# RWKV attention feeding a routed MoE on one core: TensorE's products of a unit reordered by array tiling, scores as quarters, rows from the state as column halves

## The chip, the cores and the metric

One core of one Trainium2 chip runs one program. The metric is the device time of one execution in microseconds (us). The kernel before takes 412.05 us (median of 3 runs, 411.41 to 412.96).

## The reference

```python
for t in range(S):                                   # B=4, H=8, S=768, D=48
    cur = np.einsum('bhd,bhe->bhde', u[None] * kt, vt)
    y[:, :, t] = np.einsum('bhd,bhde->bhe', rt, state + cur)
    state = wt[:, :, :, None] * state + np.einsum('bhd,bhe->bhde', kt, vt)
...
x = y.transpose(0, 2, 1, 3).reshape(B * S, H * D)    # 3072 rows of 384
logits = x @ w_gate + modality_bias[modality_id]     # 8 experts
e_idx = np.argmax(logits, axis=1)
...                                                  # gate_w: softmax value of that expert
for e in range(E):
    h = np.maximum(x[mask] @ w1[e], 0.0)             # 384 -> 1024
    out[mask] = gate_w[mask, None] * (h @ w2[e])     # 1024 -> 384
```

A recurrence over time with a decay per channel gives 3072 rows; each row then goes through the one expert that its logits choose.

## The kernel before

The sequence is cut into chunks of 128 steps. A **unit** is one chunk of one batch entry with all eight heads; there are 24, numbered n = 0 to 23, six to a batch entry. Channels lie on partitions, two heads to a tile (partitions 0 to 47 and 64 to 111), four such pairs side by side.

`att_iter(i)` (L222) works on three units at once. For unit a = i+2, VectorE (DVE) runs two scans over the decay, `B` (L230) and `E` (L233), and multiplies out `K` (L236) and `R` (L201). GpSimd (POOL) then writes `G` into the tile of `E` (L240; the profile calls it `E<-in`), after `R` has read it.

For unit m = i+1, TensorE (PE) transposes `K` into `pK` (L248), makes `delta(m)` (L213: what a step adds to its own row, four products into four column tiles of 32), the scores `pS` (L263), the state's transposed copy and update in `pU` (L273, L278), and the transposed `dl` (L280). DVE masks the scores into `A` (L269). ScalarE (ACT) copies PSUM tiles out: `KT`, `dl`, `xT`, `dT` and the state `SP`, `SPb` (L288, L291). POOL makes `dV` (L293) from `dT`. In the last unit of a batch entry there is no `pK`, no `SP` and no state update.

For unit z = i, PE makes the rows `pY` or `pX`: from the state (L303) and from the scores (L308). One iteration later DVE adds `dV` and writes `xb` (`x_rows`, L336). Two iterations later PE transposes `xb` (`x_cols`, L343) and multiplies by the gate (`logits`, L348), always into the one PSUM tile `pR_x`.

Every engine works through its own queue in the order in which the program is written (`manual_schedule`), so a waiting instruction holds up all behind it. `hooks` put extra work into an iteration after the scores: a setup at i = 4 and 5, and the routing of the first half at i = 14, 15 and 16 (`route_a`, `route_b`, `table`; the names `oh`, `tab`, `pR_x` in DVE's rows). From i = 15 to 20, POOL issues twelve scatters of `xb` (`drain`, L530), two at the end of each iteration, and at i = 18 to 20 five subtractions of the weight split (`wl`, L196) between `G` and `dV`. POOL's queue in such an iteration is `G(a)`, `wl`, `dV(m)`, scatter, scatter.

After unit 23 come the blocks of the MoE: `blk_t` (L559) transposes rows, `blk_up` (L571) and `blk_down` (L588) multiply. The last `x_rows`, `x_cols` and `logits` are put among the products of block 0.

A product's tiling follows from its operands: the rows of the array from the partitions of the operands (128, or 64 for the scores of a head), the columns from the output's partitions (128, 64 or 32). The profile prints it as rows*columns, as in `64*128`. Each fp32 product stands as two instructions.

Of the kernel before, what the change touches and what calls it, by code (L numbers as in the profile page):

```python
# [14 lines left out]
ALU = mybir.AluOpType  # L15
# [37 lines left out]
def kernel(ctx: ExitStack, tc: tile.TileContext, rkw, vt, wf, cst, mid, wg, bias, w1, w2, out):  # L53
# [107 lines left out]
    def setup_b():  # L161

        pm = pt("m", "pT")
        nc.tensor.transpose(out=pm[:, 0:NU], in_=mf, identity=ident[0:NU, 0:NU])
        m1 = cp.tile([P, 2, NU], F32, name="m1")
        nc.vector.tensor_copy(out=m1[:, 1], in_=pm[:, 0:NU])
        nc.gpsimd.tensor_scalar(out=m1[:, 0], in0=m1[:, 1], scalar1=-1.0, scalar2=1.0, op0=ALU.mult, op1=ALU.add)
# [42 lines left out]
    def delta(m):  # L210
        G, pU = T["G", m], T["pU", m]
        for p in range(4):
            nc.tensor.matmul(out=pU[32 * p:32 * p + 32, 256:384], lhsT=ub[:, p], rhs=G[:, p * P:(p + 1) * P],  # L213
                             start=True, stop=True, tile_position=(0, 32 * p))
        nc.scalar.copy(out=T["dl", m], in_=pU[:, 256:384])

# [5 lines left out]
    def att_iter(i):  # L222
# [18 lines left out]
        if ok(m):  # L241
            K, R, v = T["K", m], T["R", m], T["v", m]
            pU = pt(m, "pU")

            if not first(m + 1):
# [25 lines left out]
            cont = not first(m)  # L271
            if cont and not first(m + 1):
                nc.tensor.matmul(out=pU[:, 0:4 * D], lhsT=ident, rhs=T["SP", m].rearrange("p a b -> p (a b)"), start=True, stop=False,  # L273
                                 skip_group_check=True)
            for h in range(0 if first(m + 1) else H):
                p, hh = divmod(h, 2)
                c0 = p * P + 64 * hh
                nc.tensor.matmul(out=pU[64 * hh:64 * hh + 64, p * D:(p + 1) * D], lhsT=KT[:, c0:c0 + 64],  # L278
                                 rhs=v[:, h * D:(h + 1) * D], start=not cont, stop=True, skip_group_check=True)
# [3 lines left out]
            if not first(m + 1):  # L283
                pUv = pU[:, 0:4 * D].rearrange("p (a b) -> p a b", a=4)
# [25 lines left out]
        if ok(z - 2):  # L310
            logits(z - 2)
# [392 lines left out]
    for n, q in enumerate(seq):  # L704
# [239 lines left out]
```

## Time and profile before

| what | value |
|---|---|
| median of 3 runs | 412.05 us (411.41 to 412.96) |
| the profiled execution's own time | 411.19 us |
| its span, first to last instruction | 408.7 us |
| PE, DVE busy, share of the span | 93%, 65% |
| ACT, POOL busy, share of the span | 52%, 55% |
| mean granted TensorE clock | 0.957 |

The profiled execution lies 0.86 us under the median. Busy shares are means over two stages: the attention, up to about 174 us, where DVE and PE are both busy nearly throughout, and the MoE from there to about 401 us, where PE is. The granted clock is 1.0 at 2.4 GHz and 0.5 at 1.2 GHz.

### The profile page before, as it was taken

How to read it: one execution, taken by the hardware profiler on the slowest of the kernel's cores; microseconds unless marked ns; L12 is line 12 of the kernel's file. 1: busy time of each engine (PE TensorE's matmuls, PEld its weight loads, DVE VectorE, ACT ScalarE, POOL GpSimd, SP SyncE). 2: the span in 40 equal slices, each digit the busy share in tenths (PEclk: the TensorE clock that was granted, in tenths of full speed). 3: DMA queues.
4: the chain of work that ended last, by engine and by line, in shares of the span. 5: the costliest groups of instructions: out<-in, count | busy, mean ns of one | idle time of the engine just before them, and what ended most of it. 6: DMA issues, size and time to landing. Idle time of an engine off the chain costs nothing.

```text
span 408.7 us, 9897 instructions
## 1 busy us (share of the span) xinstructions
PE 381.1 (93%) x3807; PEld 353.6 (87%) x3807; DVE 266.5 (65%) x438; ACT 214.2 (52%) x452; POOL 224.0 (55%) x180
## 2 busy tenths in 40 slices
PE   5999979999795998999999999999999999999990
PEld 2688868888584887999999999999999999999990
DVE  5999999999988899566628684351725426471110
ACT  1354334435320554266746858777686776754320
POOL 3544263243244788158476989366484745738350
PEclk9599999999997999899999999999999999999996
DMA  7975756997636452600123653313124184146100
GB/s 155 212 161 132 166 121 128 269 248 171 157 82 153 119 136 79 197 2 1 40 59 131 239 153 119 116 42 98 54 83 132 38 289 162 40 147 194 67 28 20
DMA packets 17884, 50.46 MB, mean 123 GB/s; under 512 B 2853, under 2 KB 10571, under 8 KB 17828
## 3 DMA queue, kind: packets, MB, share of 16 engines
q1 hardware_dynamic: 14692, 40.28, 38.4%
q0 software_dynamic: 3136, 9.47, 6.4%
q8 instruction: 32, 0.52, 0.6%
q14 instruction: 24, 0.20, 0.2%
HBM read 72.89 MB, written 11.63 MB: 207 GB/s over the span
## 4 chain that ended last, share of the span: by engine, by line
PE 62%; DVE 25%; issue 5%; POOL 4%; DMA 2%; ACT 0%; SPq 0%; DVEq 0%; POOLq 0%; ACTq 0%
PE pS_u L571 23%; PE pX_d L588 12%; PE pY_d L588 12%; DVE B L230 6%; DVE E L233 5%; DVE A L269 5%; PE pS L263 3%; DVE R L201 3%; PE pR_x L348 2%; DMA in<-rkw 2%; DVE xb L336 2%; PE pK_x L559 1%; PE pT L343 1%; PE pX L308 1%; PE pX L303 1%
## 5 line engine op out<-in xcount | busy, mean ns | idle before, releaser
L196 POOL TENSOR_TENSOR wl<-raw,wh 128x768 fp32r<-128x768 f32 (+1 forms) x57 | 102.5, 1809 | 77.5 <-ACT wh L195 66.7
L195 ACT CAST wh<-raw 128x768 fp32r<-128x768 f32 (+1 forms) x104 | 83.2, 807 | 34.2 <-PE pX_d L588 24.3
L577 DVE SCALAR_TENSOR_TENSOR hl<-pS_u,hh 128x512 fp32r<-128x512 f32 x48 | 33.1, 690 | 90.7 <-ACT hh L576 90.6
L571 PE MATMUL pS_u<-xh,wh 128*128 128x256 f32 x288 | 82.0, 285 | 1.0 <-DVE hl L577 1.0
L571 PE MATMUL pS_u<-xo,wh 128*128 128x256 f32 x288 | 81.4, 283 | 0.0
L571 PE MATMUL pS_u<-xh,wl 128*128 128x256 f32 x288 | 80.9, 281 | 0.0
L240 POOL TENSOR_TENSOR E<-in 128x512 f32<-128x512 f32 x24 | 30.7, 1279 | 75.6 <-issue 23.9
L571 PEld LDWEIGHTS pS_u<-xh,wh 128*128 128x128 f32 x288 | 54.0, 188 | 1.4 <-DVE hl L577 1.4
L571 PEld LDWEIGHTS pS_u<-xh,wl 128*128 128x128 f32 x288 | 54.6, 190 | 0.0
L571 PEld LDWEIGHTS pS_u<-xo,wh 128*128 128x128 f32 x288 | 54.1, 188 | 0.0
L196 DVE TENSOR_TENSOR wl<-raw,wh 128x768 fp32r<-128x768 f32 (+1 forms) x47 | 51.2, 1089 | 2.8 <-ACT wh L195 1.8
L576 ACT ACTIVATE hh<-pS_u 128x512 fp32r<-128x512 f32 x48 | 28.8, 599 | 40.3 <-PE pS_u L571 36.4
L230 DVE TENSOR_TENSOR_SCAN B<-in,d1b 128x516 f32<-128x516 f32 x24 | 40.9, 1702 | 3.5 <-DMA in<-rkw 3.5
L596 POOL DMA_INDIRECT out<-ot,xl x25 | 32.3, 1294 | 10.9 <-ACTq L887 5.2
L588 PE MATMUL pY_d<-wh,hh 128*128 128x384 f32 x96 | 33.1, 345 | 0.0
L530 POOL DMA_INDIRECT xs<-xb,posT x24 | 28.3, 1181 | 7.9 <-issue 5.4
L263 PEld LDWEIGHTS pS<-R,K 64*128 64x128 f32 x384 | 27.3, 215 | 5.8 <-issue 4.3
L263 PE MATMUL pS<-R,K 64*128 64x128 f32 x384 | 32.3, 315 | 0.0
L269 DVE TENSOR_TENSOR A<-pS,cs 128x512 f32<-128x512 f32 x48 | 30.8, 682 | 2.2 <-PE pS L263 2.2
L588 PE MATMUL pX_d<-wh,hl 128*128 128x384 f32 x96 | 32.2, 335 | 0.0
L588 PE MATMUL pX_d<-wh,hh 128*128 128x384 f32 x96 | 32.1, 335 | 0.0
L588 PE MATMUL pX_d<-wl,hh 128*128 128x384 f32 x96 | 32.1, 335 | 0.0
(189 smaller groups left out, 751.7 us busy)
## 6 DMA issues: line engine op xcount, KB each, us to landing
raw<-w SPq DMA_DIRECT2D x56, 768.0 KB
in<-rkw SPq DMA_DIRECT2D x46, 288.9 KB
xl<-xs SPq DMA_DIRECT2D x12, 386.0 KB
v<-vt SPq DMA_DIRECT2D x24, 192.0 KB
wg<-wf SPq DMA_DIRECT2D x8, 576.0 KB
xs<-zt SPq DMA_DIRECT2D x8, 193.0 KB
out<-ot,xl POOLq DMA_INDIRECT x25, 3.1
xs<-zt SPq DMA_DIRECT2D x1, 386.0 KB
```

Of the source, the lines that this page charges most:

```text
L195: nc.scalar.copy(out=wh[k][:, sl], in_=raw[k][:, sl])
L196: (eng or (nc.vector, nc.gpsimd)[k]).tensor_tensor(out=wl[k][:, sl], in0=raw[k][:, sl], in1=wh[k][:, sl].bitcast(F32), op=ALU.subtract)
L230: nc.vector.tensor_tensor_scan(out=Bt[:, 516:0:-1], data0=w[:, 516:0:-1], data1=d1b[:, 516:0:-1], initial=0.0, op0=ALU.mult, op1=ALU.max)
L240: nc.gpsimd.tensor_tensor(out=G, in0=r, in1=k, op=ALU.mult)
L263: nc.tensor.matmul(out=pS[hh][:, p], lhsT=K[q, p], rhs=R[q, p], start=True, stop=True)
L269: nc.vector.tensor_tensor(out=A[:, hh], in0=pS[hh], in1=mask[:, None, :].to_broadcast([P, 4, P]), op=ALU.mult)
L530: rows_apart("xs", nc.gpsimd.indirect_dma_start(out=xs[:, :], out_offset=bass.IndirectOffsetOnAxis(ap=posT[:, n:n + 1], axis=0), in_=T["xb ...
L571: nc.tensor.matmul(out=pp[:, i], lhsT=wsrc[0][:, f, c * P:(c + 1) * P], rhs=xsrc[:, c], start=(n == 0), stop=(n == 3 * KC - 1))
L576: nc.scalar.activation(out=hh, in_=pp, func=AF.Relu)
L577: nc.vector.scalar_tensor_tensor(out=hl, in0=pp, scalar=0.0, in1=hh.bitcast(F32), op0=ALU.max, op1=ALU.subtract)
L588: nc.tensor.matmul(out=X["y", q][j], lhsT=hsrc[:, i, j * P:(j + 1) * P], rhs=wsrc[1][:, f], start=(f == 0 and n == 0), stop=(f == FC - 1 a ...
L596: ins = nc.gpsimd.indirect_dma_start(out=out[:, :], out_offset=bass.IndirectOffsetOnAxis(ap=xl[:, j, DM + 1:DM + 2].bitcast(I32), axis=0), ...
```

## The change

Within `att_iter`, PE's products of an iteration stand in another order: `K`'s transposes, `x_cols`, the state's copy (these with the whole array), then `delta` (128*32), the scores (now 64*64), the state update, the rows from the state and the rows from the scores (all 128*64), then the transposed `dl` and `logits` (whole array again). `x_cols` comes ahead of the scores; the transpose of `dl`, ACT's copy `dT` and POOL's `dV` come behind the rows. A score product of 64 rows by 128 columns is split into two of 64 by 64 into PSUM partitions 0 to 63 and 64 to 127, with the same 128 streamed columns (8 products become 16). A product of the rows from the state is split in the same way (4 become 8, each with 96 streamed columns). `delta` and the transposed `dl` go into the PSUM tile `pT` in place of `pU`; the setup's transpose goes into `pR_x` in place of `pT`.

```diff
@@ setup_b
-        pm = pt("m", "pT")
-        nc.tensor.transpose(out=pm[:, 0:NU], in_=mf, identity=ident[0:NU, 0:NU])
+        pm = rcol(C_VEC, NU)
+        nc.tensor.transpose(out=pm, in_=mf, identity=ident[0:NU, 0:NU])
@@ delta
-            nc.tensor.matmul(out=pU[32 * p:32 * p + 32, 256:384], lhsT=ub[:, p], rhs=G[:, p * P:(p + 1) * P],
+            nc.tensor.matmul(out=pT[32 * p:32 * p + 32, DM:], lhsT=ub[:, p], rhs=G[:, p * P:(p + 1) * P],
@@ att_iter
                 nc.scalar.copy(out=KT, in_=pK)
+            if ok(z - 2):
+                x_cols(z - 2, pT)
+
+            if cont and not last:
+                nc.tensor.matmul(out=pU[:, 0:4 * D], lhsT=ident, rhs=T["SP", m].rearrange("p a b -> p (a b)"), start=True, stop=False,
+                                 skip_group_check=True)
...
             for p in range(4):
-                for hh in range(2):
-                    q = slice(64 * hh, 64 * hh + 64)
-                    nc.tensor.matmul(out=pS[hh][:, p], lhsT=K[q, p], rhs=R[q, p], start=True, stop=True)
+                for s0 in (0, 64):
+                    for hh in range(2):
+                        q = slice(64 * hh, 64 * hh + 64)
+                        nc.tensor.matmul(out=pS[hh][s0:s0 + 64, p], lhsT=K[q, p, s0:s0 + 64], rhs=R[q, p], start=True, stop=True)
             if m == 0:
                 delta(0)
-            if ok(z - 2):
-                x_cols(z - 2)
...
-            nc.tensor.transpose(out=pU[:, 384:512], in_=T["dl", m], identity=ident)
-            dT = wt(m, "dT", [P, 4, 2])
-            nc.scalar.copy(out=dT, in_=pU[:, 384:512].rearrange("p (a b) -> p a b", a=4)[:, :, 0:2])
...
-            dV = wt(m, "dV", [P, H, D], 3)
-            nc.gpsimd.tensor_tensor(out=dV, in0=v.rearrange("p (a b) -> p a b", a=H),
-                                    in1=dT.rearrange("p a b -> p (a b)")[:, :, None].to_broadcast([P, H, D]), op=ALU.mult)
...
             if not first(z):
                 for p in range(4):
-                    nc.tensor.matmul(out=pY[:, 2 * p * D:2 * (p + 1) * D], lhsT=R[:, p], rhs=SPb[z % 3][:, p].rearrange("p a b -> p (a b)"),
-                                     start=(p == 0), stop=False, skip_group_check=True)
+                    for q in (0, 64):
+                        nc.tensor.matmul(out=pY[q:q + 64, 2 * p * D:2 * (p + 1) * D], lhsT=R[:, p, q:q + 64],
+                                         rhs=SPb[z % 3][:, p].rearrange("p a b -> p (a b)"),
+                                         start=(p == 0), stop=False, skip_group_check=True)
...
+        if ok(m):
+            pT = T["pT", m]
+            nc.tensor.transpose(out=pT[:, 0:P], in_=T["dl", m], identity=ident)
+            dT = wt(m, "dT", [P, 4, 2])
+            nc.scalar.copy(out=dT, in_=pT[:, 0:P].rearrange("p (a b) -> p a b", a=4)[:, :, 0:2])
+            dV = wt(m, "dV", [P, H, D], 3)
+            nc.gpsimd.tensor_tensor(out=dV, in0=T["v", m].rearrange("p (a b) -> p a b", a=H),
+                                    in1=dT.rearrange("p a b -> p (a b)")[:, :, None].to_broadcast([P, H, D]), op=ALU.mult)
         if ok(z - 2):
             logits(z - 2)
```

How PE's queue moves, in the iteration of unit m = 9 (after its scores, up to the next unit's transposes). Before:

```order
L343 MATMUL pT_993<-cs,xb_952 128x128 x3
L273 MATMUL pU_968<-SP_919,cs 128x192
L278 MATMUL pU_968<-v_860,KT_974 64x48 x8
L280 MATMUL pU_968<-cs,dl_976 128x128
L303 MATMUL pY_1022<-SPb_129,R_782 128x96 x4
L308 MATMUL pY_1022<-v_771,A_888 64x48 x16
L348 MATMUL pR_x<-cs,xT_994 128x8 x3
```

The same engine with the change, in the iteration of unit m = 8, from the last score product up to the next unit's first score product (the scores between are rows of the one kind):

```order
L272 MATMUL pS_8_983<-R_860,K_858 64x128
L281 MATMUL pU_960<-v_849,KT_967 64x48 x8
L300 MATMUL pX_1017<-SPb_128,R_740 64x96 x8
L306 MATMUL pX_1017<-v_729,A_884 64x48 x16
L310 MATMUL pT_961<-cs,dl_975 128x128
L354 MATMUL pR_x<-cs,xT_969 128x8 x3
L250 MATMUL pK_1068<-cs,K_955 128x128 x4
L349 MATMUL pT_1067<-cs,xb_1050 128x128 x3
L259 MATMUL pU_1066<-SP_1010,cs 128x192
L213 MATMUL pT_1067<-E_951,cs 32x128 x4
L272 MATMUL pS_9_1088<-R_957,K_955 64x128
```

`x_cols` (`pT<-cs,xb`) has moved from behind the scores to ahead of `delta` and the scores; the transpose of `dl` from ahead of both products of the rows to behind them.

ACT's queue in the iteration i = 18 (unit m = 19), before:

```order
L252 COPY KT_1964<-pK_1959 128x512
L215 COPY dl_1966<-pU_1958 128x128
L195 CAST wh_68<-raw_66 128x384 x2
L344 COPY xT_1988<-pT_1987 128x384
L282 COPY dT_2005<-pU_1958 128x8
L288 ACTIVATE SP_2007<-pU_1958,B_1948 128x48 x4
L291 COPY SPb_129<-SP_2007 64x4x48 x2
```

and with the change:

```order
L254 COPY KT_2179<-pK_2174 128x512
L350 COPY xT_2181<-pT_2173 128x384
L215 COPY dl_2187<-pT_2173 128x128
L195 CAST wh_68<-raw_66 128x384 x2
L287 ACTIVATE SP_2226<-pU_2172,B_2162 128x48 x4
L290 COPY SPb_129<-SP_2226 64x4x48 x2
L312 COPY dT_2251<-pT_2173 128x8
```

`dT`, which POOL's `dV` waits for, has moved behind the copies of the state; `xT` ahead of `dl`. POOL's own queue keeps its order (`G`, `wl`, `dV`, scatters), but for the setup's three products at i = 5, which now stand ahead of `dV`.

## Rows read from the trace of the kernel before

**Rows 1.** Busy time of each engine (us, and instructions) in two stretches of the span, the steady attention and the MoE; then granted clock, DMA share, GB/s.

```profile
16.00:106.00 90.00, 87.05 (x1309) 73.33 (x1308) 87.73 (x127) 39.29 (x134) 35.34 (x38) 0.97 0.75 177
...
174.00:401.00 227.00, 223.95 (x1615) 223.04 (x1613) 108.96 (x189) 146.04 (x229) 142.02 (x91) 1.00 0.31 101
```

**Rows 2.** All waits of DVE from 8 to 170 us: who waited for whom, us in total, times, longest.

```profile
DVE A L269 <- PE pS L263: 2.2, 3, 1.4
DVE B L230 <- DMA in<-rkw: 1.0, 1, 1.0
DVE pR_x L411 <- PE pR_x L409: 0.9, 1, 0.9
```

**Rows 3.** PE's part of one steady unit at full clock, in order of time: start, length (the ends overlap the next row's start), line, operands, tiling, instructions.

```profile
66.75 0.63 PE L248 MATMUL pK<-cs,K 128*128 128x128 f32 x4
67.32 0.43 PE L213 MATMUL pU<-E,cs 128*32 128x128 f32 x8
67.67 1.16 PE L263 MATMUL pS<-R,K 64*128 64x128 f32 x16
68.77 0.55 PE L343 MATMUL pT<-cs,xb 128*128 128x128 f32 x3
69.15 0.49 PE L273 MATMUL pU<-SP,cs 128*128 128x192 f32 x2
69.57 0.67 PE L278 MATMUL pU<-v,KT 128*64 128x48 f32 x16
70.17 0.33 PE L280 MATMUL pU<-cs,dl 128*128 128x128 f32 x1
70.34 1.03 PE L303 MATMUL pY<-SPb,R 128*128 128x96 f32 x8
71.30 1.14 PE L308 MATMUL pY<-v,A 128*64 128x48 f32 x32
72.37 0.83 PE L348 MATMUL pR_x<-cs,xT 128*128 128x8 f32 x6
73.06 0.63 PE L248 MATMUL pK<-cs,K 128*128 128x128 f32 x4
```

**Rows 4.** From the timeline of all engines about the same unit: DVE's first scan of two following units, POOL's product ahead of the first, and the load of weights that starts the state update, with its idle time before.

```profile
65.40 0.84 POOL L293 TENSOR_TENSOR dV<-v,dT 128x384 f32<-128x384 f32 x1
65.61 1.73 DVE L230 TENSOR_TENSOR_SCAN B<-in,d1b 128x516 f32<-128x516 f32 x1
...
69.57 0.55 PEld L278 LDWEIGHTS pU<-v,KT 128*64 128x64 f32 x16 [0.23 <-issue]
...
71.66 1.70 DVE L230 TENSOR_TENSOR_SCAN B<-in,d1b 128x516 f32<-128x516 f32 x1
```

**Rows 5.** PE after the routing table (i = 16 and 17): what it waits for (idle before, releaser) and when the products of the iteration start.

```profile
127.50 1.04 PE L348 MATMUL pR_x<-cs,xT 128*128 128x8 f32 x6 [4.39 <-DVE tab L470]
...
133.88 0.48 PE L280 MATMUL pU<-cs,dl 128*128 128x128 f32 x1
134.14 1.32 PE L303 MATMUL pX<-SPb,R 128*128 128x96 f32 x8
135.39 1.14 PE L308 MATMUL pX<-v,A 128*64 128x48 f32 x32
```

**Rows 6.** POOL from 134 to 164 us (first, middle and last rows of 20 that follow one another): start, length, idle before and releaser.

```profile
134.69 0.94 POOL L293 TENSOR_TENSOR dV<-v,dT 128x384 f32<-128x384 f32 x1 [1.58 <-ACT dT L282]
...
138.82 1.30 POOL L240 TENSOR_TENSOR E<-in 128x512 f32<-128x512 f32 x1
...
146.87 1.30 POOL L240 TENSOR_TENSOR E<-in 128x512 f32<-128x512 f32 x1 [0.63 <-PE pU L280]
...
162.43 1.26 POOL L240 TENSOR_TENSOR E<-in 128x512 f32<-128x512 f32 x1 [0.55 <-issue]
```

**Rows 7.** DVE in the same stretch.

```profile
133.78 1.22 DVE L230 TENSOR_TENSOR_SCAN B<-in,d1b 128x516 f32<-128x516 f32 x1
...
139.27 1.29 DVE L269 TENSOR_TENSOR A<-pS,cs 128x512 f32<-128x512 f32 x2 [1.36 <-PE pS L263]
...
140.94 2.97 DVE L230 TENSOR_TENSOR_SCAN B<-in,d1b 128x516 f32<-128x516 f32 x1
...
163.41 0.55 DVE L336 TENSOR_TENSOR xb<-pY,dV 128x384 f32<-128x384 f32 x1
```

**Rows 8.** Two stretches as in rows 1, for the granted clock (the third number from the end).

```profile
127.90:134.70 6.80, 6.80 (x55) 5.44 (x55) 6.25 (x9) 1.56 (x5) 1.28 (x2) 0.50 0.27 68
...
165.50:168.80 3.30, 3.30 (x34) 3.13 (x32) 2.29 (x4) 0.95 (x3) 0.83 (x1) 0.50 0.92 253
```

**Rows 9.** PE at the end of the attention, up to the first product of the MoE.

```profile
163.75 0.43 PE L213 MATMUL pU<-E,cs 128*32 128x128 f32 x8 [1.09 <-POOL E L240]
...
165.90 1.86 PE L303 MATMUL pY<-SPb,R 128*128 128x96 f32 x8
167.69 1.67 PE L308 MATMUL pY<-v,A 128*64 128x48 f32 x32
...
170.99 1.03 PE L303 MATMUL pX<-SPb,R 128*128 128x96 f32 x8
171.95 1.14 PE L308 MATMUL pX<-v,A 128*64 128x48 f32 x32
...
173.71 0.37 PE L571 MATMUL pS_u<-xh,wh 128*128 128x256 f32 x1
```

More of the change, by code (lines that the diff above doesn't have):

```diff
@@ L161, in setup_b @@
     def setup_b():
-        pm = pt("m", "pT")
-        nc.tensor.transpose(out=pm[:, 0:NU], in_=mf, identity=ident[0:NU, 0:NU])
+        pm = rcol(C_VEC, NU)
+        nc.tensor.transpose(out=pm, in_=mf, identity=ident[0:NU, 0:NU])
         m1 = cp.tile([P, 2, NU], F32, name="m1")
-        nc.vector.tensor_copy(out=m1[:, 1], in_=pm[:, 0:NU])
+        nc.vector.tensor_copy(out=m1[:, 1], in_=pm)
         nc.gpsimd.tensor_scalar(out=m1[:, 0], in0=m1[:, 1], scalar1=-1.0, scalar2=1.0, op0=ALU.mult, op1=ALU.add)
@@ L210, in delta @@
     def delta(m):
-        G, pU = T["G", m], T["pU", m]
+        G, pT = T["G", m], T["pT", m]
         for p in range(4):
-            nc.tensor.matmul(out=pU[32 * p:32 * p + 32, 256:384], lhsT=ub[:, p], rhs=G[:, p * P:(p + 1) * P],
+            nc.tensor.matmul(out=pT[32 * p:32 * p + 32, DM:], lhsT=ub[:, p], rhs=G[:, p * P:(p + 1) * P],
                              start=True, stop=True, tile_position=(0, 32 * p))
-        nc.scalar.copy(out=T["dl", m], in_=pU[:, 256:384])
+        nc.scalar.copy(out=T["dl", m], in_=pT[:, DM:])
     hooks = []
@@ L242, in att_iter @@
             K, R, v = T["K", m], T["R", m], T["v", m]
-            pU = pt(m, "pU")
-            if not first(m + 1):
+            pU, pT = pt(m, "pU"), pt(m, "pT")
+            last, cont = first(m + 1), not first(m)
+            if not last:
                 pK = pt(m, "pK")
@@ L260, in att_iter @@
             for p in range(4):
-                for hh in range(2):
-                    q = slice(64 * hh, 64 * hh + 64)
-                    nc.tensor.matmul(out=pS[hh][:, p], lhsT=K[q, p], rhs=R[q, p], start=True, stop=True)
+                for s0 in (0, 64):
+                    for hh in range(2):
+                        q = slice(64 * hh, 64 * hh + 64)
+                        nc.tensor.matmul(out=pS[hh][s0:s0 + 64, p], lhsT=K[q, p, s0:s0 + 64], rhs=R[q, p], start=True, stop=True)
             if m == 0:
                 delta(0)
-            if ok(z - 2):
-                x_cols(z - 2)
             for hh in range(2):
                 nc.vector.tensor_tensor(out=A[:, hh], in0=pS[hh], in1=mask[:, None, :].to_broadcast([P, 4, P]), op=ALU.mult)
[L271 to L279, printed above, removed]
-            nc.tensor.transpose(out=pU[:, 384:512], in_=T["dl", m], identity=ident)
-            dT = wt(m, "dT", [P, 4, 2])
-            nc.scalar.copy(out=dT, in_=pU[:, 384:512].rearrange("p (a b) -> p a b", a=4)[:, :, 0:2])
-            if not first(m + 1):
+            if not last:
+                for h in range(H):
+                    p, hh = divmod(h, 2)
+                    c0 = p * P + 64 * hh
+                    nc.tensor.matmul(out=pU[64 * hh:64 * hh + 64, p * D:(p + 1) * D], lhsT=KT[:, c0:c0 + 64],
+                                     rhs=v[:, h * D:(h + 1) * D], start=not cont, stop=True, skip_group_check=True)
                 pUv = pU[:, 0:4 * D].rearrange("p (a b) -> p a b", a=4)
@@ L291, in att_iter @@
                     nc.scalar.copy(out=SPb[a % 3][q, :, hh], in_=SP[q])
-            dV = wt(m, "dV", [P, H, D], 3)
-            nc.gpsimd.tensor_tensor(out=dV, in0=v.rearrange("p (a b) -> p a b", a=H),
-                                    in1=dT.rearrange("p a b -> p (a b)")[:, :, None].to_broadcast([P, H, D]), op=ALU.mult)
         elif ok(z - 2):
-            x_cols(z - 2)
+            x_cols(z - 2, pt(m, "pT"))
         if hooks:
@@ L337, in x_rows, with x_cols @@
                                 in1=T["dV", n].rearrange("p a b -> p (a b)"), op=ALU.add)
-    def x_cols(n):
+    def x_cols(n, pT):
         b, j = divmod(n, NCH)
-        pT, xT = pt(n, "pT"), wt(n, "xT", [P, DM], 2)
+        xT = wt(n, "xT", [P, DM], 2)
         for c in range(KC):
@@ L724 @@
                 if g < 2:
-                    x_cols(NU - 2 + g)
+                    x_cols(NU - 2 + g, pt(("x", g), "pT"))
                 else:
```

## The prediction

> **What bounds the kernel now.** I read the table by stages first, then DVE's waits, then one steady unit on PE and DVE, then the stretch in which the routing work is done, then the end of the attention. From 16 to 106 us DVE is busy 87.73 of 90.00 us and PE 87.05; from 174 us on PE is busy 223.95 of 227.00 us [rows 1]. The MoE's products are not touched, so the change can only move the moment at which they begin, 173.71 us [rows 9]. In the attention both engines look full, so the question is which one paces it. DVE's waits tell: from 8 to 170 us it waits for PE 2.2 us in three places at the scores and 0.9 us once at the routing, and for nothing else but one load [rows 2]. A steady unit of DVE is 6.05 us long (65.61 to 71.66, scan to scan) [rows 4]. A unit of PE is 6.31 us long (66.75 to 73.06) [rows 3]; it slips behind, but DVE needs the scores late in its own unit, and the last unit of a batch entry, with less work on PE, lets it catch up. So DVE paces the steady attention, and PE is second by little.
>
> **The change part by part.** *PE's unit.* The rows from the state take 0.96 us now (70.34 to 71.30) for 8 instructions of 96 streamed columns [rows 3]. In halves there are 16, two side by side, as the rows from the scores run. The state's copy shows the streaming: 2 instructions of 192 columns in 0.42 us with what follows them (69.15 to 69.57) [rows 3], less up to 0.1 for that, so 96 columns take 0.08 and 16 halves in pairs 8 x 0.08 = 0.66 us (my estimate; bounds: 0.96, if the pairs don't overlap better than now, and 0.53, the pace of 32 rows from the scores in 1.07 us [rows 3], which stream half as much): 0.3 us saved. The scores take 1.10 us (67.67 to 68.77) for 16 instructions of 128 columns [rows 3]; as quarters there are 32 of the same 128 columns, so only four at a time hold the 1.10. `delta` shows four column tiles at once: 8 instructions of 128 columns in 0.35 us (67.32 to 67.67) against 0.57 us for the 4 transposes before them [rows 3]. I take 1.1 us; two at a time would be 2.1. Changes of tiling fall from seven in a unit to four. One costs between 0 and the 0.23 us that the first load of the state update stands idle [rows 4]; I take 0.1, so 0.3 us. PE's unit comes to 6.31 - 0.3 - 0.3 = 5.7 us.
>
> The Trainium skill, "TensorEngine Tiling (Array Packing)", section "Theoretical Speedup", gives up to 2x for a dimension of at most 64, and multiplies for both. By that rule the scores as quarters would take half, 0.55 us; the rows above speak against it, since the split cuts no streamed column.
>
> *The steady attention.* PE's 5.7 us go under DVE's 6.05, where 6.31 were already hidden. `x_cols` now stands ahead of the scores and waits for `xb`, DVE's last product of the iteration; from there `x_cols`, the state's copy, `delta` and the scores need 0.38 + 0.42 + 0.35 + 1.10 = 2.3 us [rows 3], and DVE comes to the mask only after two scans, `K` and `R`, a full unit of 6.05 less the masks and `xb`, over 4 us. `dV` starts later, but POOL reaches it only after `G`, just before the next scan (65.40) [rows 4], and `dT` will be there. The setup's transpose in `pR_x` makes `logits` of i = 5 wait for DVE; `x_cols` behind it waits for the same iteration's `xb` anyway. Term: 0.
>
> *From the routing on.* After the table PE has waited 4.39 us and starts at 127.50 [rows 5]; its clock is 0.50 from 127.9 to 134.7 [rows 8], the lower of its two levels. Now `x_cols` delays the scores here by about 0.6 us; the fewer changes and the shorter rows give it back until the mask at 139.27, which waits 1.36 us today [rows 7]. For DVE: 0 by then. But `dT` is what counts. Its transpose starts at 133.88, and `dV` of unit 18 follows at 134.69, after POOL has waited 1.58 us for it [rows 5, 6]. With the change the transpose comes behind both products of the rows: from the state 1.25 us today (134.14 to 135.39) [rows 5], about 1.0 as halves at the mixed clock, and from the scores 1.07 [rows 3], less 0.2 for changes of tiling. So `dV` starts 1.9 us later, at 136.6. Behind it in POOL's queue stand two scatters, `G` of unit 20, two subtractions, `dV`, and so on up to `G` of unit 23 at 162.43; in these 27.7 us POOL stands idle for half a microsecond or more just twice, 0.63 and 0.55 us, both times ahead of `G` [rows 6]. If both waits swallow their full length, `G` of unit 23 is 1.9 - 1.2 = 0.7 us late; if none, 1.9. There is more to lose: the scan at 140.94 took 2.97 us beside POOL's products where one at 133.78 took 1.22 [rows 7], so POOL's products cost DVE about their own length. `G` of unit 20 (138.82, 1.30 us) lies beside DVE's wait for the scores today and costs nothing [rows 6, 7]; moved by 1.9 it meets that scan: up to 1.9 + 1.3 = 3.2. `G` waits for `R`, which comes behind these scans on DVE and moves with them, so I take 1.7, near the upper plain value. Below zero I see no way, since `dV` can't start earlier than today.
>
> *The end.* From `delta` of unit 23 (163.75) to the MoE's first product (173.71) PE is the chain, 9.96 us [rows 9]. The rows from the state stand in it twice, 1.79 us (165.90 to 167.69, at the lower clock [rows 8]) and 0.96 (170.99 to 171.95) [rows 9]; by the factor 0.66/0.96 they save 0.56 and 0.30. One transposition of tilings less: 0.1. Against it `x_cols` stands ahead of `delta` and can't start before `xb` ends at 163.41 + 0.55 = 163.96 [rows 7], 0.2 us after today's `delta`. Its own time only changes place. Net -0.7 (bounds -0.2, if the halves save half of it, and -1.2 with 0.1 more at each of five changes of tiling).
>
> **Sum:** 0 + 0 + 1.7 - 0.7 = +1.0 us. The profiled execution took 411.19 us; it lies 0.86 us under the median of the runs, so the median of the changed kernel comes to 412.05 + 1.0 = **413.0 us**; its own range, with the late POOL from 0.7 to 1.9 and 0.2 either way at the end, 411.9 to 413.4.
>
> **The rivals.** A measurement of this kernel tells about 0.5% (2.1 us) from no change: 410.0 and 414.1 are the borders.
>
> A, clearly slower: POOL's `G` meets the scan. It decides when `dV` of unit 18 starts after 140.94 - 4.13 - 1.30 = 135.5, with 4.13 the way from `dV` to `G` today [rows 6, 7]. For it: the forecast of 136.6 is past that point. Against: DVE may get its scan in ahead of `G`. Price 3.2 - 0.7 = +2.5: 414.6.
>
> B, faster: PE comes to `dT` in time, because its clock is back earlier or the halves load faster than I think. Then nothing is late at POOL, the scores' waits of 2.2 us [rows 2] shrink, the two waits of POOL of 1.2 in all [rows 6] come out, and the end gains its 0.7 and about half of what the lower clock costs there (0.83 at the rows from the state, 1.79 against 0.96 [rows 9], and as much by estimate for the rest of the stretch: 0.6 taken). -2.5: 409.5. For it: all that PE does per unit becomes shorter. Against: the wait of 4.39 us ahead of it stays, and with it the clock's fall.
>
> C, nothing but the end: the delay is swallowed by waits. -0.7: 411.4.
>
> D, the quarters run two at a time: PE's unit is 6.7 us, 0.65 over DVE's, in 15 steady units +9.8 us: 423. `delta`'s row speaks against it, though it shows column tiles alone.
>
> E, the quarters take half the time, in place of the 1.1 us that I took. `dT` comes 1.0 us earlier at the lower clock, so `G` of unit 23 is late by 0.7, and the end gains 0.55 more: 0.7 - 1.25 = -0.5: 411.5. That is the rule of "TensorEngine Tiling (Array Packing)" in the Trainium skill, cited above.
>
> **How the numbers follow.** Forecast 0.42, A 0.22, B 0.16, C 0.09, D 0.06, E 0.05. Three quarters of B lie under 410.0: faster 0.12. Most of A (0.19), D and the upper edge of the forecast (0.03) lie over 414.1: slower 0.28. The rest is 0.60. The range 410.4 to 415.2 takes in the bounds of the forecast, A, C and E, and the near edge of B; it leaves out most of B (0.13) and D (0.06).
>
> **What would show it.** In the profile after: steady scans of DVE still 6.0 us apart; a PE unit with idle time ahead of `x_cols`, the rows from the state near 0.7 us, the scores near 1.1; `dV` of unit 18 some 2 us after where it stood, and POOL's `G` of unit 23 between 163 and 166 us; from there to the MoE's first product less than the 11.28 us of today (162.43 to 173.71) [rows 6, 9]. The prediction is wrong if DVE's steady units are shorter than 5.9 us (then PE paced them after all), if `dV` of unit 18 is not late, or if the scores take 2 us.

## The result, and the profile after

The changed kernel takes 415.08 us (median of 15 runs, 412.99 to 417.99), the kernel before in the same session 411.56 (15 runs, 410.30 to 412.98): a ratio of 1.0074, 95% interval 1.0050 to 1.0097, so about 3 us slower. The forecast was 413.0 and "within 0.5%"; the time lies at the upper end of the range, 415.2, on the slower side. The profiled execution of the changed kernel took 413.10 us, 2 us under its median, so its trace shows only part of the loss: the MoE's first product starts at 175.91 us where it started at 173.71 [rows 9], 2.2 us later. No other execution of this kernel was traced; three later kernels (y1, y7 and y8), whose products and order are the same up to unit 16, show part of what slower ones do. Ratios here leave out runs over 1.5% above their kernel's fastest, and so can differ from the quotient of the medians.

Busy time by stretch, with the granted clock in the third number from the end (the first row answers to [rows 1], the last two to [rows 8]):

```profile
16.00:106.00 90.00, 80.70 (x1663) 69.15 (x1664) 87.70 (x131) 38.68 (x132) 39.45 (x41) 0.95 0.74 176
...
126.90:133.50 6.60, 5.94 (x77) 4.86 (x78) 5.06 (x9) 2.08 (x7) 1.26 (x1) 0.50 0.26 73
164.40:171.00 6.60, 5.55 (x77) 4.50 (x77) 2.94 (x5) 0.74 (x2) 0.77 (x1) 0.50 0.74 212
```

PE has 6.35 us less to do from 16 to 106 us, and DVE is as full as before. At the end of the attention 6.6 us at the lower level (1.2 GHz) stand where 3.3 stood.

PE's waits from 8 to 177 us, then DVE's from 8 to 172 (who waited for whom, us, times, longest; the second answers to [rows 2]):

```profile
PE pT L213 <- ACT xT L350: 9.8, 19, 0.8
PE pK L250 <- DVE K L236: 5.7, 2, 3.6
PE pT L349 <- DVE xb L342: 4.5, 4, 2.3
```

```profile
DVE A L276 <- PE pS L272: 6.4, 4, 3.4
DVE B L230 <- POOL E L240: 1.4, 1, 1.4
DVE pR_x L417 <- PE pR_x L415: 0.5, 1, 0.5
```

The first row is a wait that the prediction did not see. `delta` (L213) now writes into the tile `pT`, the same tile that `x_cols` (L349) has just filled, and so waits until ACT has copied `xT` out of it, 19 times. And DVE now waits 6.4 us for scores, up to 3.4 us at once, where it waited 2.2.

A steady unit on PE (start, length, idle before and releaser; answers to [rows 3]), and what DVE and POOL do about the scan of the unit before (answers to [rows 4]):

```profile
88.90 1.22 DVE L230 TENSOR_TENSOR_SCAN B<-in,d1b 128x516 f32<-128x516 f32 x1
...
94.61 1.22 DVE L230 TENSOR_TENSOR_SCAN B<-in,d1b 128x516 f32<-128x516 f32 x1
```

```profile
85.54 1.10 PE L272 MATMUL pS<-R,K 64*64 64x128 f32 x32
86.58 0.67 PE L281 MATMUL pU<-v,KT 128*64 128x48 f32 x16
87.08 0.85 PE L300 MATMUL pX<-SPb,R 128*64 128x96 f32 x16
87.75 1.09 PE L306 MATMUL pX<-v,A 128*64 128x48 f32 x32
88.77 0.33 PE L310 MATMUL pT<-cs,dl 128*128 128x128 f32 x1
...
91.31 0.43 PE L213 MATMUL pT<-E,cs 128*32 128x128 f32 x8 [0.49 <-ACT xT L350]
```

```profile
83.31 1.73 POOL L314 TENSOR_TENSOR dV<-v,dT 128x384 f32<-128x384 f32 x1 [0.28 <-ACT dT L312]
...
89.43 1.31 POOL L314 TENSOR_TENSOR dV<-v,dT 128x384 f32<-128x384 f32 x1 [0.70 <-ACT dT L312]
```

The rows from the state take 0.67 us (87.08 to 87.75), the quarters 1.04 (85.54 to 86.58). `dV` starts behind the scan's beginning (89.43 against 88.90) and no longer ahead of it; the scan then takes 1.22 us where it took 1.73, and DVE's unit is 5.71 us (88.90 to 94.61) in place of 6.05. That holds for the three units from 83.20 to 100.31 us; in the five before them `dV` still starts ahead of the scan, and they take 6.02 to 6.15 us. A whole unit of PE takes 5.63 us (140.94 to 147.06, less a wait of 0.49), where it took 6.31.

After the routing table, PE's first product (answers to [rows 5]), then POOL and DVE (answers to [rows 6] and [rows 7]):

```profile
126.05 0.83 PE L354 MATMUL pR_x<-cs,xT 128*128 128x8 f32 x6 [3.43 <-DVE tab L476]
```

```profile
135.39 1.41 POOL L314 TENSOR_TENSOR dV<-v,dT 128x384 f32<-128x384 f32 x1 [3.65 <-ACT dT L312]
...
139.52 1.30 POOL L240 TENSOR_TENSOR E<-in 128x512 f32<-128x512 f32 x1
140.76 1.96 POOL L196 TENSOR_TENSOR wl<-raw,wh 128x384 fp32r<-128x384 f32 x2
142.67 0.82 POOL L314 TENSOR_TENSOR dV<-v,dT 128x384 f32<-128x384 f32 x1
...
163.12 1.26 POOL L240 TENSOR_TENSOR E<-in 128x512 f32<-128x512 f32 x1 [0.55 <-issue]
```

```profile
131.73 1.29 DVE L276 TENSOR_TENSOR A<-pS,cs 128x512 f32<-128x512 f32 x2 [1.40 <-PE pS L272]
...
140.44 4.15 DVE L230 TENSOR_TENSOR_SCAN B<-in,d1b 128x516 f32<-128x516 f32 x1
```

`G` of unit 20 (139.52) runs when the scan wants to begin, and the scan is through at 144.59, 1.1 us after POOL's last product of that burst (142.67 + 0.82). `G` of unit 23 starts 0.69 us later than before (163.12 against 162.43): POOL's two idle spells ahead of `G` have kept their lengths (0.64 and 0.55 us, 0.63 and 0.55 before), so they swallowed nothing of the delay of `dV` of unit 18.

The end on PE (answers to [rows 9]):

```profile
164.79 0.87 PE L349 MATMUL pT<-cs,xb 128*128 128x128 f32 x3 [2.31 <-DVE xb L342]
166.32 0.65 PE L213 MATMUL pT<-E,cs 128*32 128x128 f32 x8 [0.66 <-ACT xT L350]
166.90 1.99 PE L272 MATMUL pS<-R,K 64*64 64x128 f32 x32
168.82 1.55 PE L300 MATMUL pY<-SPb,R 128*64 128x96 f32 x16
170.15 1.54 PE L306 MATMUL pY<-v,A 128*64 128x48 f32 x32
...
175.91 0.37 PE L577 MATMUL pS_u<-xh,wh 128*128 128x256 f32 x1
```

Here the new order is the chain that sets the end: `xb`, `x_cols`, ACT's `xT`, `delta`, scores, one behind the other, and it runs at half clock up to 171 us. PE had stood idle for 2.31 us ahead of it. From `G` of unit 23 to the first MoE product it is 12.79 us, where it was 11.28 and the forecast said "less than 11.28".

### The profile page after: what moved, and what is told of

Read it like the earlier page. It is cut to its first block, busy times and chain, and to the rows that moved or that the text cites. A ratio compares the mean times of both kernels' runs of the same rounds, so it can differ in the third digit from the quotient of the medians.

```text
span 410.9 us, 11025 instructions
## 1 busy us (share of the span) xinstructions
PE 371.4 (90%) x4351; PEld 346.8 (84%) x4351; DVE 266.5 (65%) x438; ACT 215.2 (52%) x452; POOL 227.3 (55%) x180
## 4 chain that ended last, share of the span: by engine, by line
PE 59%; DVE 27%; issue 5%; DMA 3%; ACT 2%; POOL 1%; SPq 0%; DVEq 0%; POOLq 0%; ACTq 0%
PE pS_u L577 23%; PE pX_d L594 12%; PE pY_d L594 12%; DVE B L230 7%; DVE A L276 5%; DVE E L233 5%; DVE R L201 3%; PE pS L272 2%; DVE xb L342 2%; DMA in<-rkw 2%; PE pR_x L354 1%; PE pK_x L565 1%; PE pU L281 1%; DMA cs<-cst 1%; PE pT L213 1%
## 5 line engine op out<-in xcount | busy, mean ns | idle before, releaser
L602 POOL DMA_INDIRECT out<-ot,xl x25 | 32.3, 1293 | 10.9 <-ACT ot L601 5.2
L314 POOL TENSOR_TENSOR dV<-v,dT 128x384 f32<-128x384 f32 x24 | 26.9, 1120 | 20.0 <-ACT dT L312 19.8
L233 DVE TENSOR_TENSOR_SCAN E<-in,d1e 128x516 f32<-128x516 f32 x24 | 31.3, 1306 | 2.4
L287 ACT ACTIVATE SP<-pU,B 128x48 f32<-128x48 f32 x80 | 17.5, 302 | 29.2 <-PE pU L281 26.7
L272 PE MATMUL pS<-R,K 64*64 64x128 f32 x768 | 31.9, 311 | 0.6 <-issue 0.6
```

Of the source, the lines that this page charges most:

```text
L233: nc.vector.tensor_tensor_scan(out=Et, data0=w[:, 0:516], data1=de, initial=0.0, op0=ALU.mult, op1=ALU.max)
L272: nc.tensor.matmul(out=pS[hh][s0:s0 + 64, p], lhsT=K[q, p, s0:s0 + 64], rhs=R[q, p], start=True, stop=True)
L602: ins = nc.gpsimd.indirect_dma_start(out=out[:, :], out_offset=bass.IndirectOffsetOnAxis(ap=xl[:, j, DM + 1:DM + 2].bitcast(I32), axis=0), ...
```

## The experiments

The theories: **1**, the shared tile `pT` makes `delta` wait for `xT`. **2**, `x_cols` waits for `xb` in front of the scores. **3**, `dV` behind the rows (3a: it is what gains in the steady units; 3b: it makes POOL late and is the loss). **4**, the waits let the granted clock fall, and that is what costs. **5**, the new shapes alone are worth nothing, since DVE paces. Each ratio is to the kernel before, run on the same chip. The changed kernel itself was run only in the session of the result; its 1.0074 is compared with ratios of later sessions.

**x1, `delta` back in `pU`** (the changed kernel otherwise).

```diff
-            nc.tensor.matmul(out=pT[32 * p:32 * p + 32, DM:], lhsT=ub[:, p], rhs=G[:, p * P:(p + 1) * P],
+            nc.tensor.matmul(out=pU[32 * p:32 * p + 32, 256:384], lhsT=ub[:, p], rhs=G[:, p * P:(p + 1) * P],
...
-        nc.scalar.copy(out=T["dl", m], in_=pT[:, DM:])
+        nc.scalar.copy(out=T["dl", m], in_=pU[:, 256:384])
```

> The changed kernel (415.1 us, ratio 1.0074 to the kernel before) with one thing put back: `delta` writes into `pU` again, a tile that ACT's copy `xT` does not read. Theory 1 (the shared tile `pT` makes `delta` wait for `xT` in front of the scores; 0.8 us between each `xT` and `delta` where it waits, 0.66 of it at the last unit): faster than the changed kernel by 0.7 to 2 us, 413.1 to 414.4, and the wait of `pT` (L213) on `xT` is gone from the list of waits. Theory 2 (what is late is `x_cols` itself, which stands ahead of the scores and waits for `xb`, 2.31 us at the last unit): 414.7 to 415.5, and A's wait of 3.36 us at the last unit stays over 2.5 us.

413.12 us against 412.63, ratio 1.0019 (0.9996 to 1.0041): about 0.55% of the 0.74% is back, and the intervals stand apart by little. PE's waits:

```profile
PE pT L349 <- DVE xb L342: 12.5, 13, 2.6
PE pK L250 <- DVE K L236: 5.4, 2, 3.7
```

The wait on `xT` is gone; PE now waits for `xb` instead, more often. A's longest wait fell from 3.4 to 1.9 us. By the time Theory 1 holds; but the first MoE product of this execution (175.89) is no earlier than in the profiled one of the changed kernel, so this pair of traces does not show where the gain lies. The traces of y1, y7 and y8 show one place, the steady units (below).

**x2, `x_cols` behind the scores.**

```diff
-            if ok(z - 2):
-                x_cols(z - 2, pT)
...
             if m == 0:
                 delta(0)
+            if ok(z - 2):
+                x_cols(z - 2, pT)
```

> The changed kernel with `x_cols` back behind the scores of its unit, and so `delta` ahead of it too; `delta` stays in `pT`. Theory 2 (`x_cols` waits for `xb` ahead of the scores): A's waits of 1.40 us at unit 18 and 3.36 us at the last unit fall below 0.7 us each, the first product of the MoE part starts 2 to 3 us earlier than at 175.91 us, and the time is 412.0 to 413.0, ratio 1.001 to 1.004. Theory 1 alone: as for the kernel with `delta` in its own tile, 413.1 to 414.4. Theory 3 (the late `dV` and POOL's `G` that meets the scan are the whole loss): 414.8 to 415.4.

412.33 us against 412.63, ratio 0.9980 (0.9961 to 0.9999): the whole loss is back, more than Theory 2 had asked for. Its profiled execution is the fastest of its 12 (408.5), so only its structure is read here. The end on PE:

```profile
163.34 0.43 PE L213 MATMUL pT<-E,cs 128*32 128x128 f32 x8 [0.48 <-POOL E L240]
163.70 1.10 PE L269 MATMUL pS<-R,K 64*64 64x128 f32 x32
164.73 0.55 PE L348 MATMUL pT<-cs,xb 128*128 128x128 f32 x3
...
171.22 0.36 PE L576 MATMUL pS_u<-xh,wh 128*128 128x256 f32 x1
```

`delta` and the scores follow `G` directly, and the 7.88 us to the MoE stand at full clock. DVE's waits ahead of the mask come to 2.0 us in all, 1.2 at the most.

**x3, `dl`'s transpose, `dT` and `dV` back ahead of the rows.**

```diff
+            nc.tensor.transpose(out=pT[:, 0:P], in_=T["dl", m], identity=ident)
...
+            dV = wt(m, "dV", [P, H, D], 3)
...
         if ok(z):
...
-        if ok(m):
-            pT = T["pT", m]
-            nc.tensor.transpose(out=pT[:, 0:P], in_=T["dl", m], identity=ident)
...
```

> The changed kernel with the transpose of `dl`, `dT` and `dV` back ahead of the rows, right behind U. Theory 3a (`dV` behind the rows is what gains in the steady units, since `dV` then starts after scan B has begun and the scan takes 1.23 us instead of 1.73): the scans of the steady units are 6.0 us apart again instead of 5.7, the 1.5 to 1.9 us gained by 110 us are gone, and the time is 415.5 to 417. Theory 3b (the late `dV` makes POOL late, `G` meets the scan at 140 us for 4.15 us, and that is the loss): the scan at 140 us is back at 3.0 us and the time is 413.4 to 414.5.

416.67 us against 412.63, ratio 1.0075 (1.0047 to 1.0103), the same as the changed kernel. The scan that took 4.15 us takes 2.95 in its profile, as 3b says, and yet nothing is won. By itself that does not rule 3b out, since a loss by 3a could cancel the gain. What rules it out as the whole loss are x5 and y6 below: the same scan takes 4.96 and 4.42 us in their profiles, and neither kernel is slower than the kernel before. 3a's extra loss is not shown: the median falls into its band, but the ratio is that of the changed kernel, and the steady units of this profile are 5.8 to 7.1 us from 72 us on, because DVE waits 2.4 us for scores there.

**x4, the two shapes alone** in the old order.

```diff
-                    nc.tensor.matmul(out=pS[hh][:, p], lhsT=K[q, p], rhs=R[q, p], start=True, stop=True)
...
+                        nc.tensor.matmul(out=pS[hh][s0:s0 + 64, p], lhsT=K[q, p, s0:s0 + 64], rhs=R[q, p], start=True, stop=True)
...
-                    nc.tensor.matmul(out=pY[:, 2 * p * D:2 * (p + 1) * D], lhsT=R[:, p], rhs=SPb[z % 3][:, p].rearrange("p a b -> p (a b)"),
...
+                        nc.tensor.matmul(out=pY[q:q + 64, 2 * p * D:2 * (p + 1) * D], lhsT=R[:, p, q:q + 64],
```

> The kernel before, in its old order, with the two new shapes alone: scores as quarters, rows from the state as column halves. Theory 5 (DVE paces the units, so the 0.3 us that the rows save on PE and the 0.07 us that the quarters save buy nothing): 411.2 to 412.1, ratio 0.999 to 1.001. Rival (the new tilings change often in the old order and each change costs about 0.1 us on PE, which shows at the end of the attention): 412.5 to 414, ratio over 1.002. Rival (quarters that stand side by side take half the time): 410.6 to 411.2.

413.24 us against 412.63, ratio 0.9998 (0.9971 to 1.0026): no difference is shown, as Theory 5 says, though the interval takes in the near edge of both rivals; the quarters' 1.04 us in the trace speaks against the second.

**p1, `x_cols` ahead alone**, in the kernel before, in a tile of its own.

```diff
+            if ok(z - 2):
+                x_cols(z - 2)
             wt(m, "dl", [P, P], 1)
             if m:
                 delta(m)
...
-            if ok(z - 2):
-                x_cols(z - 2)
```

> The kernel before with one thing changed: `x_cols` ahead of `delta` and the scores, in a tile of its own. Theory 2 (what is late is `x_cols`, which waits for `xb` in front of the scores): A's wait at the last unit grows from that of before to over 2 us, and the time rises by 1 to 3 us over the kernel before, ratio 1.0025 to 1.0075. Theory 1 (it is the shared tile that costs): 0.998 to 1.002.

The 12 runs fall in two groups, 410.1 to 413.5 and 416.2 to 418.5 us (median 414.83, before 411.36); the ratio, 1.0031 (0.9996 to 1.0065), covers the seven fastest. A's wait at the last unit is 2.29 us, as expected. In some executions this one move costs some 5 to 7 us and in others nothing or little; by the ratio alone it is unclear.

**p2, `x_cols` ahead and `delta` in its tile**, in the kernel before: as p1, and

```diff
-            pU = pt(m, "pU")
+            pU, pT = pt(m, "pU"), pt(m, "pT")
...
+                x_cols(z - 2, pT)
...
-            nc.tensor.matmul(out=pU[32 * p:32 * p + 32, 256:384], lhsT=ub[:, p], rhs=G[:, p * P:(p + 1) * P],
+            nc.tensor.matmul(out=pT[32 * p:32 * p + 32, DM:], lhsT=ub[:, p], rhs=G[:, p * P:(p + 1) * P],
```

> The kernel before with `x_cols` ahead and `delta` in the tile `pT` of `x_cols`; the shapes, U and `dV` as before. Theory 1 and 2 together (these two moves are the whole loss): ratio 1.006 to 1.009, and the wait of `delta` (L213) on `xT` stands in the list of waits with 15 to 24 entries of up to 0.8 us. Theory 2 without 1: the same as with a tile of its own. Theory 3 (the rest of the new order, `dV` behind the rows and the product from SP ahead, is what loses): 0.998 to 1.003.

421.69 us against 411.36, ratio 1.0221 (1.0176 to 1.0265): far more than expected. DVE in two steady units, and PE in the first:

```profile
65.59 1.22 DVE L230 TENSOR_TENSOR_SCAN B<-in,d1b 128x516 f32<-128x516 f32 x1
...
71.16 1.29 DVE L269 TENSOR_TENSOR A<-pS,cs 128x512 f32<-128x512 f32 x2 [1.45 <-PE pS L265]
...
72.83 1.22 DVE L230 TENSOR_TENSOR_SCAN B<-in,d1b 128x516 f32<-128x516 f32 x1
```

```profile
69.61 0.43 PE L213 MATMUL pT<-E,cs 128*32 128x128 f32 x8 [0.82 <-ACT xT L344]
```

With the old shapes PE's unit of 6.31 us [rows 3] plus the wait of 0.82 passes DVE's 6.05, and PE paces at 7.24 (65.59 to 72.83). In the changed kernel's profile the same wait is there and DVE waits for no scores from 16 to 106 us, so the shorter PE unit hides it in that execution; other executions show that it does not always (under y8). So the shorter unit earns something after all, but only part of what the change's own shared tile would cost.

**x5, both put back** (the edits of x1 and x2 together): `x_cols` behind the scores and `delta` in `pU`; shapes, the state's copy ahead and `dV` behind the rows stay.

> The changed kernel with `x_cols` behind the scores and `delta` in `pU`; the new shapes, the product from SP ahead and `dV` behind the rows stay. With `x_cols` behind, `delta` no longer stands behind a copy `xT` (Theory 1): nothing more to gain, ratio to the kernel before 0.996 to 1.000 as with `x_cols` behind alone (0.998). Rival (the tile itself costs, whatever the order, since `x_cols` then waits for the copy `dl` out of it): 0.5 to 1 us less, 0.994 to 0.997.

410.86 us against 411.36, ratio 0.9991 (0.9969 to 1.0013): nothing more than x2. With `x_cols` behind, the shared tile costs nothing. And what stays of the change is worth nothing measurable together: PE's shorter unit ends in a longer wait for POOL's `G` (10.6 us in 13 waits of `delta` from 8 to 177 us, where it was 4.4 in 6).

**y1, the changed kernel with added products.** They read ones, and nobody reads them.

```diff
+    def busy(n):
+        wp = pt(("w", n), "pK")
+        for k in range(n):
+            nc.tensor.matmul(out=wp, lhsT=wm[:, 0:P], rhs=wm, start=(k == 0), stop=(k == n - 1))
...
+            if i == NU - 2:
+                busy(9)
             if ok(z - 2):
                 x_cols(z - 2, pT)
...
+        if i == NJ + 4:
+            busy(18)
         if ok(z - 2):
             logits(z - 2)
```

> The changed kernel with added products on ones that nobody reads, where PE stands idle: 18 in unit 16 ahead of the logits, 9 in unit 22 ahead of `x_cols`. Theory 4 (the idle waits cost because the granted clock falls behind them: 0.74 in 164 to 177 us): the clock of the end is 0.9 or more, the first MoE product comes 1.5 to 2.5 us earlier, 412.6 to 413.6, ratio 1.002 to 1.005. Theories 1 and 2 alone (the waits themselves are the loss, the clock beside them costs nothing): 1.006 to 1.009. The added products in the way: over 1.009.

409.98 us against 411.36, ratio 0.9963 (0.9937 to 0.9988), beyond what Theory 4 had asked for. The waits of Theories 1 and 2 are still there (L213 on `xT` 20 times, 10.9 us; DVE for the scores 6.1 us), and the loss is gone. The added products in the wait for the table, and the clock of the two stretches (0.77 and 0.74 without them):

```profile
124.98 4.05 PE L226 MATMUL pK_('w', 18)_2016<-wm 128*128 128x512 bf16 x18
129.64 0.83 PE L364 MATMUL pR_x<-cs,xT 128*128 128x8 f32 x6 [0.61 <-DVE tab L486]
```

```profile
128.00:140.00 12.00, 10.08 (x190) 8.07 (x190) 11.40 (x25) 5.13 (x15) 5.49 (x6) 1.00 0.59 135
164.00:177.00 13.00, 11.92 (x190) 10.13 (x189) 7.21 (x13) 3.09 (x9) 2.88 (x3) 1.00 0.57 171
```

**y7 and y8, the changed kernel with one of the two places each.** y7 has the first of these lines, y8 the second:

```diff
+                busy(9)
...
+            busy(18)
```

> The changed kernel with the 9 added products in unit 22 alone, where PE waits 2.31 us for `xb` ahead of `x_cols`. If the clock of the end (0.74 in 164 to 177 us) is what the change lost: 0.999 to 1.003, most of what both places give (0.9963). If it is the clock behind the table: 1.005 to 1.008, as without.

> The changed kernel with the 18 added products in unit 16 alone, in the wait for the table. If the clock behind the table is the larger part: 0.996 to 1.002. If the clock of the end is: 1.004 to 1.008.

y7: 413.17 us against 411.46, ratio 1.0064 (1.0032 to 1.0095). y8: 411.68, ratio 1.0005 (0.9974 to 1.0035). The two stretches of y7, then of y8, and last the steady attention of y1, y7 and y8, whose code is the changed kernel's up to there:

```profile
128.00:140.00 12.00, 10.85 (x209) 9.07 (x208) 9.65 (x13) 5.78 (x18) 5.33 (x5) 0.78 0.38 91
164.00:177.00 13.00, 11.76 (x192) 10.38 (x190) 6.69 (x13) 3.68 (x10) 2.45 (x3) 1.00 0.53 158
```

```profile
128.00:140.00 12.00, 10.39 (x223) 9.07 (x224) 11.61 (x21) 6.10 (x20) 5.78 (x6) 1.00 0.52 122
164.00:177.00 13.00, 11.85 (x180) 10.87 (x181) 5.87 (x10) 2.98 (x8) 1.70 (x3) 0.87 0.52 156
```

```profile
16.00:106.00 90.00, 76.85 (x1570) 65.99 (x1570) 84.35 (x125) 37.93 (x128) 37.50 (x38) 0.96 0.74 170
16.00:106.00 90.00, 77.51 (x1622) 65.97 (x1624) 86.02 (x128) 37.54 (x126) 38.27 (x39) 0.98 0.76 177
16.00:106.00 90.00, 77.79 (x1589) 66.36 (x1592) 86.73 (x126) 37.95 (x127) 36.45 (x38) 0.96 0.79 176
```

Behind the table the clock is 1.00 in all four traces with the 18 products (y1, y2, y6, y8) and 0.50 to 0.80 in the ten without them. By the ratios that place is the larger part: 0.7% there, 0.1% at the end alone, with intervals that touch; on top of the first place, the second seems to give another 0.4% (y1 against y8, not told apart by their intervals). I had put the loss at the end, where the trace showed it; the runs put more of it 40 us earlier. (y7's profiled execution is its fastest, 411.06, so its high clock at the end need not hold for its other runs.)

The three rows of the steady attention show a place that neither the profile of the changed kernel nor my theories had. DVE is busy 84.35, 86.02 and 86.73 of the 90 us there, where it is busy 87.7 in the profiles of the changed kernel, of the kernel before and of x1, x2, x4, x5, y2 and y6: it waits for scores 3.4, 1.6 and 1.0 us. Fourteen units (the second to the sixteenth scan `B` behind 8 us) take 87.6, 85.4 and 86.2 us, against 84.4 in the profile of the changed kernel and 85.3 to 85.7 in those of the seven other kernels. So the wait on `xT` is not always hidden. By these three the 2 us between the profiled execution and the median may lie here (their mean is 2.0 over 84.4; an estimate, as the changed kernel itself has only one trace). In all of them, and in the changed kernel and x3, PE also stands idle once in the middle of the same score products, with 14 of 32 instructions left, for 0.63 to 1.73 us (they go on at 80.3 to 82.7 us); the profile names nothing that it waits for, and the cause is not shown.

**y2, the control: the same in the kernel before** (18, and 4 ahead of `delta`), and **y6, in x5** (18, and 6 there). y2's lines:

```diff
+            if i == NU - 2:
+                busy(4)
             wt(m, "dl", [P, P], 1)
...
+        if i == NJ + 4:
+            busy(18)
```

> The control for the added products: the kernel before with 18 of them in unit 16 ahead of the logits and 4 in unit 22 ahead of `delta`. Theory 4 as the cause of the loss (the change's new waits let the clock fall, and the kernel before has no such loss to give back): 0.997 to 1.002 here, against 0.9963 to 1.0074 with and without them in the changed kernel. Rival (the wait for the table, which both kernels have, 4.39 us before and 3.43 after, lets the clock fall in both, and the added products give the same back in both): 0.986 to 0.992.

> The changed kernel with `x_cols` behind the scores and `delta` in `pU` (0.9991 alone), and the added products: 18 in unit 16, 6 in unit 22 ahead of `delta`. If the waits ahead of the scores and the clock behind the table are two costs apart: 0.990 to 0.996, the fastest of all. If the added products only give back what the waits ahead of the scores took: 0.997 to 1.001.

y2: 410.31 us against 411.46, ratio 0.9976 (0.9954 to 0.9998). y6: 409.87, ratio 0.9969 (0.9946 to 0.9993). The rival, that the added products give the same everywhere, falls: 0.24% in the kernel before and 0.22% on top of x5, but 1.1% in the changed kernel. Ratios side by side:

| | without | with added products |
|---|---|---|
| before: `x_cols` behind the scores, old shapes | 1 | 0.9976 |
| x5: `x_cols` behind, new shapes | 0.9991 | 0.9969 |
| changed: `x_cols` ahead, in one tile with `delta` | 1.0074 | 0.9963 |

With the added products, the three are not told apart. The changed kernel's loss takes both: a chain that leads through PE, and a PE at half clock. That the added products act through the clock is read from the rows; no run fills the wait without raising the clock. y1, y6 and y2 are all a little faster than the kernel before, and none is shown to be the fastest.

## Why the prediction was right or wrong

The time lies just inside the range, but the likeliest class was wrong: "within 0.5%" had 0.60, "slower" 0.28. That the range holds it is luck: its upper edge stood there for a later `G`, and the time came by two other ways, the end and the clock, one of them forecast with the opposite sign and the other not at all.

**PE's unit: right.** Quarters 1.04 us (1.1 forecast), rows from the state 0.67 (0.66), the whole unit 5.63 (5.7). Rivals D and E fall. The Trainium skill, "TensorEngine Tiling (Array Packing)", section "Theoretical Speedup", gives up to 2x for a dimension of at most 64, from which 0.55 us for the quarters was the estimate. That stretched it: the split dimension of the scores is 128, and only the pieces are 64. The trace shows 1.04, against 1.10 undivided [rows 3]. My reason, that the split leaves the streamed columns as they were, is not enough: it leaves them so in the rows from the state too, and these gained 0.29 us. Why the one split gains and the other does not is not shown.

**The steady attention: no term of 0 that can be relied on, and two sentences behind it are wrong.** The sign that I had named against myself came, DVE's units of 5.71 us; not because PE had paced them, but because `dT` was not there in time and `dV` slipped behind the scan. The lead did not last: scan `B` is 1.91 us earlier at 108.25 than its counterpart at 110.16, 0.38 at 133.40 [rows 7] and later from 148 us on. In the profiles of x1 and x2, with `dV` behind the rows as here, the units are 6.0 us again, so it takes the waits of PE as well. And `delta`'s new tile, which I gave no price, brought a wait of up to 0.8 us per unit that needs the shorter PE unit as its cover; p2 shows the price without it, and y1, y7 and y8 show DVE waiting for the scores even with it.

**From the routing on: right in sign, wrong in its working.** `dV` of unit 18 is 0.70 us late (135.39 against 134.69 [rows 6]), not 1.9, because PE reached the table's products 1.45 us sooner (126.05 against 127.50 [rows 5]). Then rival A's mechanism came all the same: `G` met the scan, which took 4.15 us against 2.97 [rows 7], +1.18. `G` of unit 23 came out +0.69, where +1.7 was forecast: the late `dV` came through at its full 0.70. The meeting is not the loss, since x5 and y6 have it too and lose nothing. The scan ended 1.1 us after POOL's burst did, about its own length: it waited and did not share. The Trainium skill, "SBUF — State Buffer", section "SBUF: two separate sides", says of the port pair of DVE and GpSimd, for a DVE instruction with two SBUF inputs against a GpSimd one that reads SBUF: whoever starts first has it for the whole instruction, and the other blocks. The trace agrees that one blocks; but three of POOL's products that began after the scan was due (140.76 and later, against 140.44) went ahead of it, which that sentence does not explain.

**The end: the failed step.** Forecast -0.7, measured +1.51 (12.79 against 11.28). The four pieces, an estimate across traces of several kernels, with the chain at full clock from the control y2 (`delta` to MoE 8.40 us), x2 and x5 (7.88) and y7 (`x_cols` to MoE 8.58). The first and last rows of that chain in y2, then in y7:

```profile
165.66 0.42 PE L213 MATMUL pU<-E,cs 128*32 128x128 f32 x8
...
174.06 0.37 PE L581 MATMUL pS_u<-xh,wh 128*128 128x256 f32 x1
```

```profile
165.23 0.52 PE L357 MATMUL pT<-cs,xb 128*128 128x128 f32 x3 [0.58 <-DVE xb L350]
...
173.81 0.37 PE L585 MATMUL pS_u<-xh,wh 128*128 128x256 f32 x1
```

| piece | us |
|---|---|
| new shapes and what else stays in x2 and x5, 7.88 - 8.40 | -0.52 |
| `x_cols` and the copy `xT` ahead of `delta`, 8.58 - 7.88 | +0.70 |
| half clock: (11.12 - 8.58) - (9.96 - 8.40) | +0.98 |
| start: `x_cols` 1.67 behind `G`, `delta` was 1.32 | +0.35 |

The saving was as forecast (-0.7, bounds -0.2 and -1.2): the rows from the state save 0.46 (168.82 to 170.15) and 0.25 us (173.49 to 174.20), 0.56 and 0.30 forecast. What failed is the sentence that the time of `x_cols` "only changes place": it changed place from beside the chain into it, with ACT's copy behind it, and the chain then ran at half clock for twice as long. The forecast's own range, too, gave the end 0.2 us either way where its bounds stood 0.5 apart on each side. The sum of the profiled pair is +0.69 + 1.51 = 2.20 us, which is all of its delay.

**The clock.** I took the two stretches of low clock over from the trace of before as fixed. The runs show that their cost depends on what waits for PE: the added products in unit 16 give 0.7% in the changed kernel (y8) and, with those of unit 22, 0.24% in the one before. The traces show it in DVE's two units behind the table: 14.07 us in the changed kernel (126.37 to 140.44) and 11.45 in y8, 13.20 before (127.74 to 140.94) and 11.57 in y2. The lower clock costs 2.6 us there in the new order and 1.6 in the old, 1.0 us more. No term of the sum held that.

**Open.** Why the clock falls in one execution of a kernel and not in another (p1's two groups); what slows the changed kernel's other executions beside the waits in the steady units; why PE stands idle in the middle of the scores at 80 us; how much of x1's gain is the wait itself and how much the clock behind it; whether the added products act by the clock alone; what the state's copy ahead, the halves and the quarters are worth one by one.

## What to carry to other kernels

A move that groups instructions for one engine also moves each of them ahead of others in its queue: ask of every moved instruction what it waits for, and what stood behind nothing before and now stands behind it. Two results in one PSUM tile are one dependency: a writer waits for the reader of the other half. Where TensorE's granted clock falls after a wait, as here to 0.50 behind the wait for the table, the wait costs more than its length: try the same kernel with idle time filled before you blame the order. And one profiled execution is not the kernel: later traces with the same code up to unit 16 show waits that the first one does not have.

## What the runs showed of the hardware that was not expected

- Nobody reads the 18 products of 128x512 (4.05 us) in PE's wait for the table; the granted clock from 128 to 140 us rises from 0.77 to 1.00, and with 9 more at the end the kernel runs 1.1% faster.
- The same scan of 128x516 takes 1.22 us when POOL's `dV` begins after it, 1.73 when it begins just before [rows 4], and 4.15 when it meets a burst of four POOL products, ending 1.1 us after the last.
- A unit's score products on the 64*64 tiling, 32 instructions, take 1.04 us at full clock and 1.92 at half (166.90 to 168.82).
